# First projection of an MLP in four of six column pairs by seven block products instead of eight

## The chip, the cores and the metric

The kernel runs on one core of a Trainium2 chip. The metric is the device time of one execution in microseconds (us). Five engines work beside each other: TensorE (PE: matmuls; its weight loads are a separate row, PEld), VectorE (DVE), ScalarE (ACT), GpSimd (POOL) and SyncE (SP, which here only issues loads). DMA engines move data and can add into memory while they write ("accumulating" DMA).

## The reference

Three stages, all in float32, for B=2 batches of S=576 tokens (1152 tokens in all) with 8 heads of 64:

```python
# stage 1: linear attention, phi(x) = concat(exp(p), exp(-p)), p = x@w_phi - max|x@w_phi|
kv = einsum('bhsf,bhsd->bhfd', k_p, v);  z = sum(k_p, axis=2)
x = einsum('bhsf,bhfd->bhsd', q_p, kv) / (einsum('bhsf,bhf->bhs', q_p, z)[..., None] + 1e-06)
# stage 2, "first MLP": x [1152, 512], d_ff = 1536
x = (x @ w_a * (x @ w_b)) @ w_out
# stage 3, "second MLP": 4 experts, F = 1024, p = probs normalized over experts
for e in range(4):
    out += p[:, e:e + 1] * (maximum(x @ w1[e], 0) @ w2[e])
```

## The kernel before

**Precision.** A matmul takes its operands in fp32r. Each operand is therefore split into a high part (a copy by ACT that rounds, `high`) and a low part (what is left over, `low`), and a product is three matmuls: high·high, high·low, low·high. The low part is either a subtraction on DVE or POOL, or ("M") a negated copy on ACT followed by an accumulating DMA issued by POOL (L146 and L147).

**Weights.** w_a, w_b and w_out come as 64-bit words that carry float64 values. SP loads them in small pieces (L445); ACT takes magnitude and rest (L467, L468), DVE clamps, shifts and joins them (L475, L478, L481), POOL adds (L484). Then come the high part (L134) and the low part (L135, POOL, or L147). The weights of the second MLP are float32 and need only sums and splits.

**First MLP.** d_ff is cut into six pairs of 256 columns (j = 0 to 5). Pairs 0, 1, 4 and 5 run in halves of 288 tokens: `unit_ab` does w_a (ACT copies the bank to `a`, L755 multiplies by the bank of w_b into `gg`), the product is split into `hhb` (L761 is its low part on DVE), and `o1` (L778 to L780) does the projection back with w_out, which DVE adds to `part` (L672). Pairs 2 and 3 run in blocks of 384 tokens (`block_ab`, L805 to L807, and `block_o`, L834 to L836). Every projection here is plain: all 2×2×2 block products.

**Second MLP.** Also in pairs (j = 0 to 15) and two halves tp of 576 tokens, named unit (j, tp). The first projection goes by seven block products (a Strassen-like scheme): `unit` (L664 to L666) makes products M1 to M7 in banks X, Y, Z from block sums of weights (`wc`) and of x (`xc`, made once by `sums_x`, L383 and L386). ACT copies a bank (L669), DVE adds a bank to the copy (L672), and X is accumulated on in place, so a product into X waits until ACT has copied it. The second projection (L978 to L980) goes by seven too, with sums of h (L918), and DVE accumulates the result times p (L986); pairs in EXCEPT, and only halves named there, are done plainly (L1023 to L1025).

**What sets the order.** TensorE's order is the order of the program's loops: a unit yields after each block product, and `run` puts queued work of the projection back between. The preparation of weights is a list of tasks, of which so many are taken after each product as the tables RATES, TASKS and BEFORE say. In the attention the string SCRIPT orders everything. Each engine runs its own list in order, so an instruction that waits holds back all behind it on that engine.

**Memory at the change of stage.** The order of the last units of the first MLP is (4,0), (5,0), (4,1), then `unit_h(0, 0)` of the second MLP, then (5,1). Only then are the pools of the first MLP released and the second buffer of `wc` and the sums of x for tp = 1 allocated (`l_p`):

```python
        xt_p.release()
        w_p.release()
        ga_p.release()
        l_p = ctx.enter_context(tc.tile_pool(name="l", bufs=1, side="left", reuse_waits="tile"))
        xc[1] = l_p.tile([128, 2, 7, 2, HT], F32R, tag="xc", name="xc")
        wc_t.append(l_p.tile([128, 2, 7, 256], F32R, tag="wc", name="wc"))
```

Of the kernel before, what the change touches and what calls it, by code (L numbers as in the profile page):

```python
# [18 lines left out]
NT = B * S  # L19
# [9 lines left out]
S2 = (0, 1)  # L29
EXCEPT = ((15, 1), (15, 0))  # L30
SUMS_H = "PPDP"
LOW_H = "DDMDDD"
LOW_P = "MDP"
SUMS_1 = "DDDP"
SUMS_2 = "DDPD"
LOW_1 = "PMM"
LOW_2 = "MMMM"
LATE = (4, 6, 9, 9, 11, 12, 12)
SUMS_H1 = "PPDP"
LOW_H1 = "DDPDDD"  # L40
LATE1 = (1, 1, 2, 3, 4, 6, 8)
BEFORE1 = (0, 3, 4, 0, 4, 0, 4, 3, 8, 3, 5, 6, 10, 7, 4, 4)
RATE = 1.8
CAP = 1.6
PLAIN2 = 9
RATE0 = 0.9
RATE9 = 1.4
RATES = (1.3, 1.3, 1.4, 1.8, 2.7)
TASKS0 = (1, 0, 5, 0, 4, 1, 0, 0, 0, 1, 0, 1, 0, 2)
TASKS = (0, 1, 1, 4, 4, 1, 0, 0, 1, 1, 1, 1, 1, 1)  # L50
BEFORE = (0, 2, 4, 3, 4, 3, 2, 3, 8, 5, 5, 7, 10, 0, 1, 4)
PLAIN = (0, 4, 1)
# [26 lines left out]
def tile_linear_attention_then_mlps(ctx, tc, qT, kT, v, w_phi, wab, wout, w12, probs, out):  # L79
# [17 lines left out]
    ab_p = ctx.enter_context(tc.tile_pool(name="ab", bufs=1, side="left"))  # L97
    w_p = tc.alloc_tile_pool(name="w", bufs=1, side="left")
# [7 lines left out]
    ga_p = None  # L106
    l_p = None
# [14 lines left out]
    with tc.manual_schedule():  # L122
# [13 lines left out]

        def engine(by):
            return nc.gpsimd if by == "P" else nc.vector

        def high(hi, src):  # L140
            nc.scalar.activation(out=hi, in_=src, func=AF.Copy)  # L141

        def low(by, lo, src, hi):

            if by == "M":
                nc.scalar.activation(out=lo, in_=src, func=AF.Copy, scale=-1.0)  # L146
                nc.gpsimd.dma_start(out=lo, in_=src, accum_op=ALU.add)  # L147
            else:
                engine(by).tensor_tensor(out=lo, in0=src, in1=hi.bitcast(F32), op=ALU.subtract)  # L149
# [223 lines left out]
        def stage_xparts(b, c, x):  # L373
            xf = x.rearrange("p a b -> p (a b)")
            hi, lo = (t[:, c, S * b:S * b + S] for t in xs)
            nc.scalar.activation(out=hi, in_=xf, func=AF.Copy)
            nc.gpsimd.tensor_tensor(out=lo, in0=xf, in1=hi.bitcast(F32), op=ALU.subtract)

        def sums_x(b, a, second):
# [4 lines left out]

            def high(k, n, src):
                nc.scalar.activation(out=o[:, 0, k:n, a, :], in_=src, func=AF.Copy)  # L386

            def low(k, n, src):
                sub(nc.vector, o[:, 1, k:n, a, :], src, o[:, 0, k:n, a, :].bitcast(F32))

            x, o = part[b][:, a], xc[b]
            end = (b, a) == (B - 1, 1)
            if not second:
                tt[b, a] = m_p.tile([128, 4, HT], F32, tag="g", name="t", bufs=3)
                sub(nc.vector if end else nc.gpsimd, tt[b, a][:, 0], x[:, 0], x[:, 1])
                return
# [25 lines left out]

        raws = {}
        units = []
        for j in range(FP1):
            units += [("ab", 2 * j), ("ab", 2 * j + 1), ("o", j)]
        f64 = [(u, f) for u in units for f in range(2)]
        for j in range(FP2):
            units += [("1", j), ("2", j)]
        f64_next = [0]  # L430

        def load_raw():

            if f64_next[0] >= len(f64):
                return
            u, f = f64[f64_next[0]]
            f64_next[0] += 1
            t = w_p.tile([128, 1024], U32, tag="raw", name="raw", bufs=2)
            src = {"ab": wab, "o": wout}[u[0]][u[1]]
            src = src[:, 512 * f:512 * f + 512].bitcast(U32)  # L440
            if u[0] == "ab":
                for n in range(4):
                    for d in range(2):
                        r = 64 * (n % 2) + 32 * d
                        nc.sync.dma_start(  # L445
                            out=t[32 * n:32 * n + 32].rearrange("p (a d x) -> p a d x", a=2, d=2)[:, :, d],
                            in_=src[r:r + 32].rearrange("p (a e x) -> p a e x", a=2, e=2)[:, :, n // 2],
                        )
            else:
                nc.sync.dma_start(out=t, in_=src)  # L450
            raws[u, f] = t

        w_t = {}
        state = {}


        SPARE = [("ab", FA - 6), ("ab", FA - 5)]

        def begin(k):

            rv = raws[f64[k]].rearrange("p (n t) -> p n t", t=2)
            lo, hi = rv[:, :, 0], rv[:, :, 1]
            m = w_p.tile([128, 512], U32, tag="m", name="m", bufs=2)
            r = w_p.tile([128, 512], U32, tag="rn", name="rn", bufs=2)
            nc.scalar.activation(out=m.bitcast(F32), in_=hi.bitcast(F32), func=AF.Abs)  # L467
            nc.scalar.activation(out=r, in_=lo, func=AF.Copy, scale=2.0 ** -29)  # L468
            state[k] = hi, m, r

        def middle(k):
            hi, m, r = state[k]
            x = w_p.tile([128, 512], U32, tag="wx", name="wx", bufs=2)
            mf = m.bitcast(F32)
            nc.vector.tensor_scalar(  # L475
                out=mf, in0=mf, scalar1=bits(0x38000000), scalar2=bits(0x47EFFFFF), op0=ALU.max, op1=ALU.min
            )
            nc.vector.tensor_scalar(  # L478
                out=m, in0=m, scalar1=3, scalar2=0x3FFFFFFF, op0=ALU.logical_shift_left, op1=ALU.bitwise_and
            )  # L480
            nc.vector.scalar_tensor_tensor(  # L481
                out=x, in0=hi, scalar=0xC0000000, in1=m, op0=ALU.bitwise_and, op1=ALU.bitwise_or
            )
            nc.gpsimd.tensor_tensor(out=x, in0=x, in1=r, op=ALU.add)  # L484
            state[k] = x.bitcast(F32)
            load_raw()

        def parts(k):
            u, f = f64[k]
            if u in SPARE:  # L490
                if u not in w_t:
                    t = m_p.tile([128, 2, 2, 2, 512], F32R, tag="xc", name="w")
                    w_t.update((s, t[:, i]) for i, s in enumerate(SPARE))
            elif f == 0:
                if u[0] == "ab":
                    w_t[u] = ab_p.tile([128, 2, 2, 512], F32R, tag=f"ab{ab_turn[0] % 4}", name="w")
                    ab_turn[0] += 1
                else:
                    w_t[u] = od_p.tile([128, 2, 2, 512], F32R, tag="o", name="w", bufs=2)
            two_parts(w_t[u][:, 0, f], w_t[u][:, 1, f], state.pop(k), nc.gpsimd)  # L500

        stage_t = {}
        ab_turn = [0]

        def load_w(u):


            def go():
                if u == ("1", 0):
                    stage_t[u] = [w_p.tile([128, 4, 256], F32, tag="raw", name="wt", bufs=2) for _ in range(2)]  # L510
                    t = stage_t[u][0]
                elif u[0] == "1":
                    home = 3 if len(S2) == 2 or u[1] % 2 else 1
                    t = ab_p.tile([128, 8, 256], F32, tag=f"ab{home}", name="wt")
                    stage_t[u] = t[:, 0:4], t[:, 4:8]
                else:
                    big = ab_p.tile([128, 8, 256], F32, tag="ab2", name="wx")
                    t = big[:, 0:4].rearrange("p (f h) n -> p f (h n)", f=2)
                    stage_t[u] = t, big
                for f in range(2):  # L520
                    src = w12[2 * u[1] + f]
                    if u[0] == "1":
                        o = t[:, 1:3] if f == 0 else t[:, 0:4:3]
                        for h in range(2):
                            nc.sync.dma_start(
                                out=o[:, h].rearrange("p (a n) -> p a n", a=2),
                                in_=src[:, 0:512].rearrange("p (a h n) -> p h a n", h=2, a=2)[:, h],
                            )
                    else:
                        nc.sync.dma_start(out=t[:, f], in_=src[:, 512:1024])  # L530
            return go

        def sum_w(u, k):
            def go():
                if u[0] == "2":
                    b11, b12, b21, b22, t0, t1, t2, t3 = (stage_t[u][1][:, n] for n in range(8))
# [704 lines left out]
```

## Time and profile before

| | |
|---|---|
| median of three runs | 689.53 us (689.14 to 691.02) |
| profiled execution | 691.6 us, its span 689.7 us |
| instructions | 15326 |
| PE busy | 679.0 us, 98% of the span |
| DVE / ACT / POOL busy | 542.8 (79%) / 427.6 (62%) / 334.9 (49%) us |

The span is the time between the first and last instruction on the core; what lies around it is 1.9 us here. Matmuls overlap each other in the records: one of 288 columns is shown as 0.29 us long, while the next starts 0.13 us later. So the cost of a matmul is read from start to start, not from its length. The attention takes about the first 90 us, the first MLP the time to about 335, the second MLP the rest.

### The profile page before, as it was taken

The numbers are of one execution on the slowest core, as the hardware profiler recorded it, in microseconds if no ns is written. First come the engines' busy times: TensorE is split into PE (matmuls) and PEld (weight loads), VectorE is DVE, ScalarE is ACT, GpSimd is POOL, SyncE is SP. The second block draws the span as 40 slices with busy tenths as digits, with TensorE's granted clock in tenths as the row PEclk, the third lists the DMA queues.
The fourth block names the chain that finished last, engine by engine and source line by source line (L and its number), as shares of the span: only waits on it lengthen the run. The fifth ranks groups of instructions, "written<-read, shape, count | busy, mean of one in ns | idle before, by whom it ended". The sixth has DMA issues, their size and how long they took to land.

```text
span 689.7 us, 15326 instructions
## 1 busy us (share of the span) xinstructions
PE 679.0 (98%) x5706; PEld 653.9 (95%) x5706; DVE 542.8 (79%) x1175; ACT 427.6 (62%) x907; POOL 334.9 (49%) x354
## 2 busy tenths in 40 slices
PE   9998999999999999999899999999999999999998
PEld 8995679999999999999799999999999999999996
DVE  6889964547565567564649999999999999999985
ACT  5767855454444353433597777777686868777761
POOL 1211664334443344511256756665665667565730
PEclk9999999999999999999999999999999999999999
DMA  6742232223322232211257656665656666665654
GB/s 196 211 130 69 59 98 62 68 86 82 105 73 80 92 93 62 62 31 32 40 122 139 132 112 127 128 129 114 129 122 120 129 133 119 125 126 115 124 85 153
DMA packets 63499, 72.63 MB, mean 105 GB/s; under 512 B 7296, under 2 KB 43456, under 8 KB 63424
## 3 DMA queue, kind: packets, MB, share of 16 engines
q0 software_dynamic: 15552, 26.48, 22.9%
q1 hardware_dynamic: 47648, 45.00, 21.9%
q8 instruction: 45, 0.74, 0.5%
q14 instruction: 30, 0.25, 0.1%
q10 hardware_dynamic: 224, 0.16, 0.1%
HBM read 42.78 MB, written 2.36 MB: 65 GB/s over the span
## 4 chain that ended last, share of the span: by engine, by line
PE 93%; DVE 4%; ACT 1%; issue 1%; DMA 1%; SPq 0%; DVEq 0%
PE kv L276 5%; PE ab L748 5%; PE X L665 5%; PE X L666 5%; PE ab L750 5%; PE ab L749 5%; PE X L664 5%; PE X L980 4%; PE X L978 4%; PE X L979 4%; PE num L343 3%; PE acc L779 3%; PE acc L780 2%; PE acc L778 2%; PE Z L666 2%; PE Z L664 2%
## 5 line engine op out<-in xcount | busy, mean ns | idle before, releaser
L986 DVE SCALAR_TENSOR_TENSOR oacc<-X,pr,oacc 128x256 f32<-128x256 f32 x224 | 97.1, 474 | 5.4 <-PE X L980 5.2
L484 POOL TENSOR_TENSOR wx<-wx,rn 128x512 uint32<-128x512 uint32 x36 | 46.5, 1291 | 92.1 <-DVE wx L481 92.1
L918 POOL TENSOR_TENSOR h<-h 128x256 f32<-128x256 f32 x56 | 44.5, 794 | 82.3 <-DVE h L918 49.6
L135 POOL TENSOR_TENSOR w<-wx,w 128x512 fp32r<-128x512 f32 x36 | 47.9, 1332 | 70.5 <-ACT w L134 70.5
L665 PE MATMUL X<-xc,wc 128*128 128x288 f32 x256 | 75.7, 296 | 0.0
L748 PE MATMUL ab<-xh,w 128*128 128x288 f32 x256 | 75.7, 296 | 0.0
L666 PE MATMUL X<-xc,wc 128*128 128x288 f32 x256 | 75.5, 295 | 0.0
L750 PE MATMUL ab<-xh,w 128*128 128x288 f32 x256 | 75.4, 295 | 0.0
L749 PE MATMUL ab<-xl,w 128*128 128x288 f32 x256 | 75.4, 294 | 0.0
L664 PE MATMUL X<-xc,wc 128*128 128x288 f32 x256 | 75.3, 294 | 0.0
L669 ACT ACTIVATE h<-X 128x288 f32<-128x288 f32 x64 | 26.3, 410 | 69.7 <-PE X L666 69.7
L141 ACT ACTIVATE hhs<-h 128x256 fp32r<-128x256 f32 (+2 forms) x146 | 65.1, 475 | 0.3 <-DVE h L918 0.2
L147 POOL DMA_DIRECT2D w<-wx x60 | 51.9, 877 | 26.1 <-ACT w L146 16.2
L980 PE MATMUL X<-w,hhs 128*128 128x256 f32 x224 | 63.2, 282 | 0.2 <-DVE hhs L149 0.2
L978 PE MATMUL X<-w,hhs 128*128 128x256 f32 x224 | 62.8, 280 | 0.2 <-DVE oacc L986 0.2
L979 PE MATMUL X<-w,hhs 128*128 128x256 f32 x224 | 62.9, 281 | 0.0
L149 DVE TENSOR_TENSOR hhs<-h,hhs 128x512 fp32r<-128x512 f32 x114 | 60.4, 529 | 0.8 <-ACT hhs L141 0.8
L672 DVE TENSOR_TENSOR part<-acc,part 128x288 f32<-128x288 f32 (+2 forms) x80 | 34.7, 452 | 31.6 <-PE acc L836 18.6
L986 DVE SCALAR_TENSOR_TENSOR oacc<-Z,pr,oacc 128x256 f32<-128x256 f32 x112 | 48.8, 476 | 8.1 <-PE Z L980 7.1
L664 PEld LDWEIGHTS X<-xc,wc 128*128 128x128 f32 x256 | 48.3, 189 | 0.3
L665 PEld LDWEIGHTS X<-xc,wc 128*128 128x128 f32 x256 | 48.2, 188 | 0.4
L748 PEld LDWEIGHTS ab<-xh,w 128*128 128x128 f32 x256 | 48.0, 188 | 0.5 <-issue 0.5
(153 smaller groups left out, 2386.5 us busy)
## 6 DMA issues: line engine op xcount, KB each, us to landing
w<-wx POOLq DMA_DIRECT2D x60, 256.0 KB, 4.3
raw<-in_wab SPq DMA_DIRECT2D x192, 64.0 KB, 2.1
wt<-in_w SPq DMA_DIRECT2D x64, 128.0 KB, 2.6
wc<-wt POOLq DMA_DIRECT2D x32, 256.0 KB, 3.3
wx<-in_w SPq DMA_DIRECT2D x32, 256.0 KB, 3.1
raw<-in_wout SPq DMA_DIRECT2D x12, 512.0 KB, 3.7
xraw<-in_qT SPq DMA_DIRECT2D x6, 384.0 KB, 4.0
v<-in_v SPq DMA_DIRECT2D x8, 256.0 KB, 5.2
```

The costliest lines, as they stand in the source:

```text
L141: nc.scalar.activation(out=hi, in_=src, func=AF.Copy)
L149: engine(by).tensor_tensor(out=lo, in0=src, in1=hi.bitcast(F32), op=ALU.subtract)
L664: nc.tensor.matmul(out=ps, lhsT=whi, rhs=xhi, start=first and a == 0, stop=False, skip_group_check=True)
L665: nc.tensor.matmul(out=ps, lhsT=whi, rhs=xlo, start=False, stop=False, skip_group_check=True)
L666: nc.tensor.matmul(out=ps, lhsT=wlo, rhs=xhi, start=False, stop=a == 1, skip_group_check=True)
L748: nc.tensor.matmul(out=t, lhsT=whi, rhs=hi, start=(c == 0), stop=False)
L749: nc.tensor.matmul(out=t, lhsT=whi, rhs=lo, start=False, stop=False)
L750: nc.tensor.matmul(out=t, lhsT=wlo, rhs=hi, start=False, stop=(c == KD - 1))
L978: nc.tensor.matmul(out=t[:, p], lhsT=hi, rhs=whi, start=st, stop=False, skip_group_check=True)
L979: nc.tensor.matmul(out=t[:, p], lhsT=hi, rhs=wlo, start=False, stop=False, skip_group_check=True)
L980: nc.tensor.matmul(out=t[:, p], lhsT=lo, rhs=whi, start=False, stop=True, skip_group_check=True)
L986: nc.vector.scalar_tensor_tensor(out=o, in0=t[:, p], scalar=pr[:, i, e:e + 1], in1=o, op0=ALU.mult, op1=ALU.add)
```

## The change

Four of the six pairs of the first MLP (2 to 5) make x @ w_a by seven block products with `unit`, the code of the second MLP. For that the attention stage is followed by block sums of x (`sums_t`: four differences per 288-token plane, split in high and low), and each of these pairs' w_a gets four block sums (`split`). w_b stays plain, pairs 0 and 1 stay plain. The 384-token blocks are gone: all units are halves of 576 tokens in two 288-token parts. In a pair the order is a of half 0, a of half 1, b of half 0, b of half 1; in the last pair a, b of half 0 and then a, b of half 1. `unit_h(0, 0)` comes after both.

Memory is laid out anew: two staging buffers (`st_p`), three buffers wA, wB and wC for loads and conversion, one home `wc_t[0]` for w_a and one `wc_t[1]` for w_b, which become the two `wc` buffers of the second MLP. Low parts of converted weights are now nearly all made with the accumulating DMA (LOWS). Preparation is a list per engine (tables PLAIN, POPS, ENG, H00). In the second MLP fewer low parts of h are made on DVE and more by accumulating DMA (LOW_H, LOW_H1), and unit (1, 0) joins EXCEPT: its second projection is plain. SCRIPT orders the attention stage otherwise, with eight instead of nine conversions before the last piece of x.

```diff
-EXCEPT = ((15, 1), (15, 0))
+SEVEN = {1: "", 2: "a", 3: "a", 4: "a", 5: "a"}
+SUMS = {"a": "DDDD", "b": "PPDP", "1": "DDPP", "2": "DDDP"}
+LOWS = {"a": "MMD", "b": "MMD", "1": "DMM", "o": "MM", "2": "PMMM"}
...
+EXCEPT = ((15, 1), (15, 0), (1, 0))
...
+        def minus(o, i, e):
+
+            if e == "M":
+                nc.scalar.activation(out=o, in_=i, func=AF.Copy, scale=-1.0)
+
+        def rest_of(o, i, hi, e):
+            if e == "M":
+                nc.gpsimd.dma_start(out=o, in_=i, accum_op=ALU.add)
+            else:
+                by[e].tensor_tensor(out=o, in0=i, in1=hi.bitcast(F32), op=ALU.subtract)
...
+            raws = [wide["wA"][:, 0:1024], wide["wA"][:, 1024:2048], wide["wB"][:, 0:1024]]
+            ms = [wide["wB"][:, 1024 + 512 * n:1536 + 512 * n] for n in range(2)]
+            ms += [wide["wC"][:, 512 * n:512 * n + 512] for n in range(2)]
+            return raws[k % 3], ms[k % 4]
...
+            if m in "ab":
+                gate = (m, j - 1) if j > 1 else "m" if m == "b" else None
+            s = []
+            for k in range(4):
...
+                h = op("A", u, high(lo, hi, LOWS[m][n]), *after, gate=gate)
...
+                q = late_op(LOWS[m][n], u, low(lo, hi, LOWS[m][n]), h)
+                last = [q] if n == 0 else last + [q]
...
+                tt["x", b, a] = x, t
+                xh, xl = planes()[:2]
+                nc.vector.tensor_tensor(out=x, in0=xh.bitcast(F32), in1=xl.bitcast(F32), op=ALU.add)
+
+            def diff(k):
+                def go():
+                    x, t = tt["x", b, a]
+                    i, j = ((x[:, 0], x[:, 1]), (x[:, 2], x[:, 0]), (x[:, 2], t[:, 0]), (x[:, 3], t[:, 2]))[k]
+                    by[DIFFS[k]].tensor_tensor(out=t[:, k], in0=i, in1=j, op=ALU.subtract)
+                return go
+
...
-            w, x = w_t[u], xc[tp]
+            w, x = w_t[u], (xq[tp], xt[tp], u[0] != "1")
...
+        def unit_a(j, tp):
+            if "a" not in SEVEN[j]:
+                return unit_pa(j, tp)
+            need(("t", tp))
+            c = ca[tp] = new_c("a")
+            return unit(("a", j), tp, c, nothing, nothing, lambda X: copy(c[:, 1, HT:], X))
...
-        order = [(0, 0), (1, 0), (0, 1), (1, 1)] + [(j, n) for j in BLOCKS for n in range(NTB)]
-        order += [(FP1 - 2, 0), (FP1 - 1, 0), (FP1 - 2, 1), None, (FP1 - 1, 1)]
-        for jt in order:
-            if jt is None:
-                run(unit_h(0, 0), 1.2, RATES[4])
-                continue
-            j, tp = jt
-            if j in BLOCKS:
...
-        l_p = ctx.enter_context(tc.tile_pool(name="l", bufs=1, side="left", reuse_waits="tile"))
-        xc[1] = l_p.tile([128, 2, 7, 2, HT], F32R, tag="xc", name="xc")
-        wc_t.append(l_p.tile([128, 2, 7, 256], F32R, tag="wc", name="wc"))
-        w2_t.extend(l_p.tile([128, 8, 256], F32R, tag=f"w2{k}", name="w") for k in range(2))
...
+        run(unit_plain(1), 1.0, PLAIN)
+        for j in range(1, FP1):
+            for m, tp in (("a", 0), ("a", 1), ("b", 0), ("b", 1)) if j < FP1 - 1 else (("a", 0), ("b", 0), ("a", 1), ("b", 1)):
+                k = m if m in SEVEN[j] else m.upper()
+                run((unit_a if m == "a" else unit_b)(j, tp), R5 if (j, tp) == (FP1 - 1, 1) else POPS[k], ENG[k])
+                if j == FP1 - 1 and m == "b":
+                    fresh(tp, True)
+        assert not any(t == 0 for q in queue for t, l, h in q[1])
```

GpSimd at the passage from the first to the second MLP, before: `wt_3873` are the staged weights of pair 1 of the second MLP, `wc_4146` their split home, `t_4182` sums of x for tp = 1.

```order
L543 TENSOR_TENSOR wt_3873<-wt_3873 128x256
L383 TENSOR_TENSOR t_4182<-part_2183 128x288
L383 TENSOR_TENSOR t_4182<-part_2183,t_4182 128x288 x2
L149 TENSOR_TENSOR wc_4146<-wt_3873,wc_4146 128x768
L147 DMA wc_4146<-wt_3873 128x512 x2
L543 TENSOR_TENSOR wx_4070<-wx_4070 128x256
L147 DMA w_4148<-wx_4070 128x512 x4
```

The same place now; `wt_4118` and `wc_1616` are the staged and split weights of that pair, and `t_4186` are the last sums of x.

```order
L375 TENSOR_TENSOR t_3964<-part_1619,t_3964 128x288 x2
L375 TENSOR_TENSOR t_4019<-part_1619 128x288
L375 TENSOR_TENSOR t_4019<-part_1619,t_4019 128x288 x2
L447 DMA wc_105<-wt_3399 128x512 x2
L666 TENSOR_TENSOR wt_4118<-wt_4118 128x256 x2
L375 TENSOR_TENSOR t_4186<-part_1959 128x288
L375 TENSOR_TENSOR t_4186<-part_1959,t_4186 128x288 x2
L447 DMA wc_1616<-wt_4118 128x512 x2
L776 TENSOR_TENSOR wt_4123<-wt_4123 128x256
```

The two DMAs into the home of pair 1 now stand behind the sums of x for tp = 1 and two weight sums, with no subtraction of 768 columns before them.

ScalarE at that place before; `h_4266` is the copy of unit (0, 0), `h_4335` of unit (0, 1).

```order
L669 ACTIVATE h_4266<-X_4267 128x288
L141 ACTIVATE wc_4146<-wt_3873 128x768
L669 ACTIVATE h_4266<-Z_4269 128x288
L872 ACTIVATE hhb_1578<-h_4266 128x288
L141 ACTIVATE wc_4146<-wt_3873 128x512
L146 ACTIVATE wc_4146<-wt_3873 128x512
L872 ACTIVATE hhb_1578<-h_4266 128x576
L872 ACTIVATE hhb_1578<-X_4267 128x288
L141 ACTIVATE wc_4146<-wt_3873 128x512
L146 ACTIVATE wc_4146<-wt_3873 128x512
L669 ACTIVATE h_4335<-X_4336 128x288
```

And now; `h_4106` is unit (0, 0), `oacc_4258` belongs to the second projection of unit (0, 0), and `h_4301` is unit (0, 1).

```order
L883 ACTIVATE h_4106<-X_4107 128x288
L883 ACTIVATE h_4106<-Z_4109 128x288
L677 ACTIVATE wc_1616<-wt_4118 128x768
L1136 ACTIVATE hhb_1530<-h_4106 128x288
L1136 ACTIVATE hhb_1530<-h_4106 128x576
L381 ACTIVATE xq_4104<-part_1959 128x3x288
L677 ACTIVATE wc_1616<-wt_4118 128x512
L443 ACTIVATE wc_1616<-wt_4118 128x512
L1136 ACTIVATE hhb_1530<-X_4107 128x288
L381 ACTIVATE xt_4105<-t_4186 128x4x288
L677 ACTIVATE wc_1616<-wt_4118 128x512
L443 ACTIVATE wc_1616<-wt_4118 128x512
```

The last split of the weights of pair 1 (L146 before, L443 now) stood directly ahead of the first copy of unit (0, 1). Now two splits of x and two rows of `oacc` follow it, and only then the first copy of unit (0, 1), `h_4301`.

VectorE in pair 2, before: `gg` and `hhb` of one block, `part` of the projection back.

```order
L672 TENSOR_TENSOR part<-acc,part 128x384
L475 TENSOR_SCALAR m<-m 128x512
L478 TENSOR_SCALAR m<-m 128x512
L481 SCALAR_TENSOR_TENSOR wx<-raw,m 128x512
L812 TENSOR_TENSOR gg<-ab,a 128x384
L817 TENSOR_TENSOR hhb<-gg,hhb 128x384
L672 TENSOR_TENSOR part<-acc,part 128x384 x2
```

And now in pair 3, with names as before; `c<-Y`, `c<-X`, `c<-Z` are additions of the seven-product unit.

```order
L886 TENSOR_TENSOR part<-acc,part 128x288 x3
L582 SCALAR_TENSOR_TENSOR wB<-wA,wB 128x512
L886 TENSOR_TENSOR part<-acc,part 128x288 x2
L563 TENSOR_SCALAR wB<-wB 128x512
L569 TENSOR_SCALAR wB<-wB 128x512
L886 TENSOR_TENSOR c<-Y,c 128x288
L449 TENSOR_TENSOR hhb<-c,hhb 128x576
L886 TENSOR_TENSOR part<-acc,part 128x288
L582 SCALAR_TENSOR_TENSOR wB<-wB 128x512
L886 TENSOR_TENSOR part<-acc,part 128x288
L886 TENSOR_TENSOR c<-X,c 128x288
L886 TENSOR_TENSOR c<-Z,c 128x288
```

Between two conversions (three instructions each) there now stand additions of the unit and of the projection back mixed.

## Rows read from the trace of the kernel before

**Rows 1.** Busy time (count) by engine in stretches, granted clock, DMA share, GB/s.
```profile
50.00:64.00 14.00, 11.55 (x208) 8.55 (x204) 13.12 (x24) 11.47 (x28) 2.57 (x2) 1.00 0.30 95
...
160.00:170.00 10.00, 9.55 (x59) 9.10 (x58) 6.01 (x8) 4.64 (x9) 4.69 (x4) 1.00 0.35 93
170.00:290.00 120.00, 120.00 (x782) 120.00 (x782) 74.78 (x150) 52.89 (x96) 53.01 (x43) 1.00 0.30 84
...
330.00:341.00 11.00, 8.93 (x62) 8.29 (x62) 8.86 (x17) 8.08 (x16) 4.19 (x4) 1.00 0.14 25
341.00:345.00 4.00, 4.00 (x16) 3.41 (x16) 0.76 (x2) 0.41 (x1) 0.13 (x1) 0.58 0.53 113
...
368.00:686.00 318.00, 318.00 (x2429) 312.49 (x2428) 299.15 (x726) 228.81 (x520) 193.06 (x231) 1.00 0.60 124
```

**Rows 2.** Groups by line and shape: TensorE; busy us, mean ns, idle before.
```profile
L748 PE MATMUL ab<-xh,w 128*128 128x288 f32 x256 | 75.7, 296 | 0.0
...
L778 PE MATMUL acc<-hhb,w 128*128 128x288 f32 x128 | 37.9, 296 | 0.1
...
L805 PE MATMUL ab<-xh,w 128*128 128x384 f32 x96 | 32.2, 336 | 0.0
...
L834 PE MATMUL acc<-hhb,w 128*128 128x384 f32 x48 | 16.0, 334 | 0.0
```

**Rows 3.** Timeline of TensorE: start, duration, line, operation.
```profile
299.80 0.29 PE L664 MATMUL Z<-xc,wc 128*128 128x288 f32 x1
...
302.98 0.29 PE L664 MATMUL Z<-xc,wc 128*128 128x288 f32 x1
...
230.34 0.34 PE L805 MATMUL ab<-xh,w 128*128 128x384 f32 x1
...
233.49 0.34 PE L805 MATMUL ab<-xh,w 128*128 128x384 f32 x1
...
341.65 0.63 PE L1023 MATMUL acc<-w,hhb 128*128 128x512 f32 x1
...
344.21 0.38 PE L664 MATMUL X<-xc,wc 128*128 128x288 f32 x1
...
677.92 0.39 PE L1023 MATMUL acc<-w,hhs 128*128 128x512 f32 x1
...
684.72 0.28 PE L1023 MATMUL acc<-w,hhs 128*128 128x256 f32 x1
...
686.03 0.28 PE L1025 MATMUL acc<-w,hhs 128*128 128x256 f32 x1
```

**Rows 4.** Chain that ended last, 334 to 347 us: start, us, what.
```profile
336.55 0.53 ACT wc L146
...
337.36 3.32 DMA wc<-wt
...
340.72 0.41 PE Z L666
```

**Rows 5.** Groups by line and shape: GpSimd and ScalarE.
```profile
L147 POOL DMA_DIRECT2D w<-wx x60 | 51.9, 877 | 26.1 <-ACT w L146 16.2 <-PE Z L980 3.2 <-issue 3.1
...
L669 ACT ACTIVATE h<-X 128x288 f32<-128x288 f32 x64 | 26.3, 410 | 69.7 <-PE X L666 69.7
...
L543 POOL TENSOR_TENSOR wt<-wt 128x256 f32<-128x256 f32 x16 | 14.4, 902 | 2.6 <-DVE wt L543 2.6
```

**Rows 6.** Timeline of VectorE, then of GpSimd, from 155.7 us.
```profile
155.71 0.42 DVE L475 TENSOR_SCALAR m<-m 128x512 f32<-128x512 f32 x1
...
157.66 1.36 DVE L475 TENSOR_SCALAR m<-m 128x512 f32<-128x512 f32 x1
...
157.45 1.27 POOL L484 TENSOR_TENSOR wx<-wx,rn 128x512 uint32<-128x512 uint32 x1 [5.62 <-DVE wx L481]
```

**Rows 7.** DMA issues: tile, engine, count, KB each, median us to landing.
```profile
w<-wx POOLq DMA_DIRECT2D x60, 256.0 KB, 4.3
...
wc<-wt POOLq DMA_DIRECT2D x32, 256.0 KB, 3.3
```

More of the change, by code (lines that the diff above doesn't have):

```diff
@@ L421, in tile_linear_attention_then_mlps @@
         kept_low = []
+        ticks = [0]
         raws = {}
[L424 to L451, printed above, removed]
@@ L453, in tile_linear_attention_then_mlps @@
+        f64 = [((m, j), f) for j in range(FP1) for m in "abo" for f in range(2)]
+        f64.sort(key=lambda uf: (uf[0][1], "abo".index(uf[0][0]), uf[1]))
+        late = [(m, j) for j in range(FP2) for m in "12"]
         w_t = {}
         state = {}
[L457 to L469, printed above, removed]
@@ new lines, in tile_linear_attention_then_mlps, with place, freed, op @@
+        uses = {}
+        recent = {"st": [], "raw": []}
+        bufs = {"st": 2, "m": 4, "raw": 3}
+        made = {}
+        m_rel = {}
+        def place(tag, k):
+            made[tag] = k
+            return k
+        def freed(tag):
+            return recent[tag][-bufs[tag]] if len(recent[tag]) >= bufs[tag] else None
+        def op(e, u, fn, *after, gate=None):
+            ops.append((u, fn, [a for a in after if a is not None], gate, e))
+            line[e].append(len(ops) - 1)
+            return len(ops) - 1
@@ new lines, in ready, with emit, prep @@
+        def ready(k, steps):
+            u, fn, after, gate, e = ops[k]
+            free = gate is None or (m_p is not None if gate == "m" else uses[gate] == 0)
+            return free and all(a in at and (at[a] + steps * (2 if ops[a][4] == "S" or a in slow else 1) <= ticks[0] or ops[a][4] == e) for a in after)
+        def emit(k):
+            ops[k][1]()
+            at[k] = ticks[0]
+        def prep(engines):
+            for e in engines + "XXSS":
+                k = next((k for k in line[e] if ready(k, 1)), None)
+                if k is not None:
+                    line[e].remove(k)
+                    emit(k)
@@ L505, in load_w @@
         def load_w(u):
             def go():
[L509 to L519, printed above, removed]
+                t = st_p.tile([128, 8, 256], F32, tag="st", name="wt", bufs=2)
@@ L599, in tile_linear_attention_then_mlps @@
-        t_next = [0]
-        before = {}
-        for kinds, n in (("ab",), 4), (("o", "2"), 2):
-            same = [u for u in units if u[0] in kinds and u not in SPARE]
-            before.update({u: same[i - n] for i, u in enumerate(same) if i >= n})
-        before["load", "2", 0] = ("ab", FA - 4)
-        before["load", "1", 1] = ("ab", FA - 3)
-        before["load", "2", 1] = ("ab", FA - 2)
-        before["load", "1", 2] = ("ab", FA - 1)
-        for j in range(2, FP2):
-            before["1", j] = ("1", j - 2)
@@ L611, in tile_linear_attention_then_mlps @@
[L611 to L628 removed]
+                second(u, l, gate)
@@ L827, in block_o @@
[L827 to L842 removed]
+        left = {}
```

768 lines of the change are left out of this document (481 added, 287 removed).

## The prediction

> **What bounds the kernel now.** I read the stretches of the span first, because a change in the first MLP has its price there and not in the mean over the span. TensorE is busy for all of the 120 us from 170 to 290 and for all of the 318 us from 368 to 686 [rows 1]. In these stretches only fewer or shorter matmuls can save time. The reader should look for the stretches in which it is not full: 50 to 64 us, where VectorE is busy 13.12 of 14 us and TensorE 11.55; 160 to 170 (0.45 us idle); and 330 to 341 (2.07 us idle), behind which lie 4 us at a granted clock of 0.58 [rows 1]. Then I read the groups by shape for the number of matmuls [rows 2], the timeline for what each costs from start to start [rows 3], and the chain for what the idle 2 us wait for [rows 4].
>
> The costs by [rows 3]: 24 steps of 288 columns lie between 299.80 and 302.98, 0.1325 us each; 18 of 384 columns between 230.34 and 233.49, 0.175 us; 30 of 512 between 677.92 and 684.72, 0.2267 us; 11 of 256 between 684.72 and 686.03, 0.119 us.
>
> **Term 1, the matmuls: -5.2 us.** One pair's x @ w_a by halves is 4 token parts × 2 column blocks × 4 row blocks × 3 = 96 matmuls of 288 columns. By seven products it is 84. Four pairs save 48, and 48 × 0.1325 = 6.4 us. The 384-column work is 3 × 96 + 3 × 48 = 432 matmuls [rows 2], 75.6 us at 0.175; the same columns as 576 matmuls of 288 cost 76.3, so +0.7. Unit (1, 0) of the second MLP loses 42 matmuls of 256 columns (5.0 us) and gets 24 of 512 (5.4), so +0.4. All this lies on an engine that was full, so it counts in full: -6.4 + 0.7 + 0.4 = -5.3, or -5.2 without rounding in between. If TensorE stays full, this term can't come out otherwise.
>
> **Term 2, the passage to the second MLP: -3.8 us.** In the chain ScalarE ends the last split of pair 1's weights at 337.08, GpSimd issues the accumulating DMA, that takes 3.32 us, and TensorE's product Z starts at 340.72 [rows 4]. The wait is the 2.07 us of the stretch. After it the clock is at the lower level for part of 341 to 345: mean 0.58 of full, that is 4 × 0.42 = 1.7 us lost, and six matmuls of 512 columns take 2.56 us from 341.65 to 344.21, 0.43 each in place of 0.227 [rows 1, 3]. Fully granted it is 2.4 GHz; 0.43 is what the level of 1.2 GHz gives. Both together are 3.8 us. The weights came late because their home was free only when the first MLP's buffers were released. Now the home of w_b becomes that buffer, and is free after the last w_b unit. The split is written inside unit (0, 0), and in ScalarE's and GpSimd's lists the DMA stands well ahead of unit (0, 1): by the matmuls in between (some 40 of 288 columns and 24 of 512 of the plain part: 5.3 + 5.4 = 10.7 us), some 10 us for a DMA that lands in 3.3 us [rows 7]. Bounds: 0 (another wait takes its place, with the same dip of the clock) to -3.8. I take -3.8, since both the wait and the work ahead of it are in rows.
>
> **Term 3, the attention: -0.4 us.** From 50 to 64 us VectorE is the bound [rows 1]. The new order has one conversion fewer there on VectorE and one clamp on GpSimd; the clamp alone is 0.42 us [rows 6]. What else the conversions saved there is done later beside matmuls. At most the 2.45 us idle in that stretch can go; at worst GpSimd's clamp, with no row of its own, takes as long as its other operations on 512 columns, 1.27 us [rows 6], and is waited for, +1.3. I take the clamp.
>
> **Term 4, new waits in the first MLP: +0.6 us.** VectorE gets more work: its instructions of the first MLP go from 219 to 304. It was busy 74.8 of 120 us with 150 instructions, 0.50 us each [rows 1]; 85 more are 42 us over the some 235 us of that stage, so its share goes from 62% to about 80%. ScalarE was at 44% and gains the block sums' splits and the negated copies; I put these at a third of its work, which makes some 60%. Neither is full, but a seven-product unit has a shorter rope than a plain one: product M6 or M7 goes into the bank that ScalarE must have copied, with one product Y (6 × 0.1325 = 0.8 us) and at times a projection back (another 0.8) in between, and the copy takes 0.41 [rows 5]. A ScalarE instruction that waits for a raw load and stands ahead of the copy holds it back; behind the copy wait VectorE's additions and then TensorE. The eight units of pairs 2 to 5 are bounded by nothing at all below and by a wait like that of the passage, 2.07 us each, above: 0 to 16.6 us. The nearest row for a wait in the middle of this stage is 160 to 170, 0.45 us for one [rows 1], with VectorE's stretched conversion in front of it. I take one matmul, 0.13 us, per unit, 1.0 in all, less the 0.45 of that place whose order is gone: +0.6.
>
> **Term 5, the second MLP: 0.** TensorE is full there; GpSimd was busy 193 of 318 us [rows 1]. It now issues 146 accumulating DMAs rather than 106, 40 × 0.877 = 35 us more, and makes 45 weight sums rather than 29, 16 × 0.90 = 14 us more [rows 5]; what else moves about cancels. That makes 242 of some 318 us, 76%. VectorE falls from 299 us by about as much as it makes fewer low parts, so its 94% goes down. The cover is TensorE's own work: a pair of units is some 21 us long (318 us for 15 pairs), while GpSimd has some 16 us to do in it. Bounds: 0 to +15 (second rival).
>
> **Sum.** -5.2 - 3.8 - 0.4 + 0.6 = -8.8. Of the profiled execution's 691.6 us (span 689.7) that leaves 682.8 (span 680.9). That execution lies 2.1 us above the median of the runs, 689.53, so for the median I expect 680.7, and say 681.
>
> Where VectorE and GpSimd meet, the trace speaks against the change: a clamp of 0.42 us took 1.36 us when it started at 157.66, inside a GpSimd operation that ran from 157.45 to 158.72 [rows 6]; it ended 0.30 us after that one. The Trainium skill, "SBUF — State Buffer", section "SBUF: two separate sides", says that the two engines take a shared pair of ports as an exclusive lock for a whole instruction, and warns that a DMA issued by GpSimd waits for its descriptors while VectorE holds it. The row agrees with the first half; no run here shows the second. By this rule the 40 added DMA issues of the second MLP would be slowed too, and the time would come out as in the second rival.
>
> **Rivals.**
> (a) The passage's wait only moves. Unit (0, 1) then waits for sums of x or for other weights, and the clock dips again. For it: the last sums of x for half 1, partly on GpSimd, can begin only after the last projection back, and VectorE was busy 8.86 of 11 us there [rows 1]. Against it: all other weights are issued early. Time: 689.5 - 5.2 - 0.4 + 0.6 = 684.5; with half of it back, 682.6.
> (b) Slower: low parts that come late in the second MLP. Place: the second projection of each unit, whose low parts of h now come in more cases by a DMA that GpSimd issues behind sums and other DMAs. A DMA lands 3.3 to 4.3 us after its issue [rows 7], where VectorE passes over 512 columns in 0.42 us (its clamp) [rows 6]. If GpSimd falls behind by the stretching seen in [rows 6], the price is about half a microsecond in each of some 29 units, +14.5, and the time 695.2. It decides from 8.8 / 29 = 0.3 us per unit. Against it: GpSimd has a quarter of its time free, and the projection is not asked for until some products later.
> (c) Waits eat the gain of the first MLP. At a microsecond in each of eight units in place of 0.13, term 4 is 7.6, and the time 687.7; with two, it is about 695, slower as well. For it: VectorE at 80% with conversions that hold up additions; against it: four banks, and TensorE full through 120 us with VectorE at 62% [rows 1].
>
> **How the numbers follow.** Forecast (677.5 to 683.5): 0.55. Rival (a) (683.5 to 686.5): 0.20. Rival (c): 0.13, of which 0.07 within 0.3% of 689.53 (2.07 us, about what can be told from no change), 0.03 on either side. Rival (b): 0.12, of which 0.11 slower and 0.01 the same. So faster is 0.55 + 0.20 + 0.03 = 0.78, the same 0.08, slower 0.14. The range is 677 to 689: its low end has the attention's whole 2.45 us and no new waits (689.5 - 5.2 - 3.8 - 2.5 = 678) and another microsecond for stretches that I count full; its upper end takes in (a) and the first half of (c).
>
> **What would show it.** Right: 336 seven-product matmuls in the first MLP at 0.13 us each; no wait of TensorE for `wc` near the passage, and a clock of 1.0 there; TensorE full from the start of the second MLP on, GpSimd at about three quarters. Term 4 shows as idle time of TensorE before products into X and Z with ScalarE or VectorE as the one that ended it. The prediction is wrong if TensorE's idle time within the second MLP is above 2 us, or if the clock is lowered anywhere else, since a dip costs as much again as the wait ahead of it.

## The result and the profile after

The changed kernel took 683.38 us (median of 4 runs, 682.83 to 684.04), the kernel before 689.5 us in the runs beside it. The ratio is 0.9907, 95% interval 0.9889 to 0.9926, a gain of 6.1 us. It is faster, inside the stated range, and 2.4 us above the 681 us forecast. In the two profiled executions the span fell from 689.7 to 681.1 us, by 8.6 us, close to the 8.8 us of the sum. So the question is not where a large gain went, but why the traces show 8.6 us and the medians some 6, and whether the terms are right one by one.

The head of the page of the changed kernel: busy time, share of the span, instructions.

```profile
span 681.1 us, 15846 instructions
## 1 busy us (share of the span) xinstructions
PE 671.9 (99%) x5784; PEld 646.5 (95%) x5784; DVE 574.2 (84%) x1159; ACT 458.4 (67%) x990; POOL 389.3 (57%) x425
```

The same kernel by stretches, with columns as in [rows 1] (PE, PEld, DVE, ACT, POOL, granted clock, DMA share, GB/s). The second MLP ends some 9 us earlier than before (its last matmul starts at 677.33 instead of 686.03), so 330 to 366 holds the passage, and 370 to 677 answers to 368 to 686.

```profile
50.00:64.00 14.00, 12.18 (x212) 8.54 (x212) 12.70 (x22) 11.57 (x28) 0.00 (x0) 1.00 0.23 65
160.00:170.00 10.00, 10.00 (x77) 10.00 (x76) 5.99 (x14) 4.91 (x10) 3.44 (x4) 1.00 0.71 152
170.00:290.00 120.00, 120.00 (x906) 120.00 (x905) 91.29 (x182) 59.32 (x110) 43.24 (x38) 1.00 0.52 120
330.00:366.00 36.00, 36.00 (x230) 33.24 (x229) 21.27 (x40) 28.43 (x64) 23.85 (x28) 1.00 0.52 99
366.00:370.00 4.00, 2.89 (x24) 2.69 (x23) 3.90 (x8) 2.83 (x7) 4.00 (x6) 1.00 0.99 192
370.00:677.00 307.00, 307.00 (x2337) 301.15 (x2337) 285.61 (x635) 226.22 (x531) 240.62 (x283) 1.00 0.67 125
```

TensorE is full through the first MLP and through the passage, at full clock: the 2.07 us wait and the dip of [rows 1, 4] are gone. VectorE rose from 62% to 76% in 170 to 290, GpSimd from 61% to 78% in the second MLP. But a new hole of 1.11 us stands at 366 to 370. The chain of waits in that place (start, us, what) shows what it is:

```profile
363.29 0.37 POOL xq L447
363.66 0.16 issue
363.82 5.40 DMA hhs<-h
369.21 0.04 issue
369.26 0.39 PE Z L1243
```

The low part of a block of h, made by an accumulating DMA, lands 5.40 us after its issue, and the third matmul of product Z waits for it. When it is issued, two others of the same queue are still under way: one with weights (w, 256 KB), which lands 0.08 us later, and one for other blocks of h (xq, 128 KB). And 0.34 us behind it SyncE issues two loads of the next weights (256 KB each); from 366 to 370 us the DMA engines are 99% busy (the share 0.99 above). That is the place of rival (b), in one unit of some 29.

```profile
364.16 1.06 SPq L762 DMA_DIRECT2D wt<-in_w  x2
```

### The profile page after: what moved, and what is told of

The parts are those of the page before. It is cut to its first block, busy times and chain, and to the rows that moved or that the text cites. A ratio compares the mean times of both kernels' runs of the same rounds, so it can differ in the third digit from the quotient of the medians.

```text
span 681.1 us, 15846 instructions
## 1 busy us (share of the span) xinstructions
PE 671.9 (99%) x5784; PEld 646.5 (95%) x5784; DVE 574.2 (84%) x1159; ACT 458.4 (67%) x990; POOL 389.3 (57%) x425
## 4 chain that ended last, share of the span: by engine, by line
PE 89%; DMA 3%; POOL 2%; SPq 2%; DVE 2%; ACT 1%; issue 1%; POOLq 0%; ACTq 0%; DVEq 0%
PE X L879 6%; PE X L880 6%; PE X L878 6%; PE ab L1029 4%; PE acc L1089 4%; PE ab L1031 4%; PE acc L1088 4%; PE ab L1030 4%; PE acc L1087 4%; PE X L1242 4%; PE X L1241 4%; PE X L1243 4%; PE Z L878 3%; PE Z L879 3%; PE Z L880 3%; PE num L336 2%
## 5 line engine op out<-in xcount | busy, mean ns | idle before, releaser
L878 PE MATMUL X<-xt,wc 128*128 128x288 f32 x240 | 71.0, 296 | 0.0
L879 PE MATMUL X<-xt,wc 128*128 128x288 f32 x240 | 70.8, 295 | 0.0
L880 PE MATMUL X<-xt,wc 128*128 128x288 f32 x240 | 70.8, 295 | 0.0
L447 POOL DMA_DIRECT2D hhs<-h x41 | 57.3, 1398 | 12.6 <-ACT hhs L443 10.4
L447 POOL DMA_DIRECT2D wc<-wt x40 | 35.5, 889 | 45.4 <-ACT wc L443 25.7
L1029 PE MATMUL ab<-xq,wc 128*128 128x288 f32 x192 | 56.8, 296 | 0.0
L1089 PE MATMUL acc<-hhb,w 128*128 128x288 f32 x192 | 56.8, 296 | 0.0
L1030 PE MATMUL ab<-xq,wc 128*128 128x288 f32 x192 | 56.7, 295 | 0.0
L1088 PE MATMUL acc<-hhb,w 128*128 128x288 f32 x192 | 56.7, 295 | 0.0
L1031 PE MATMUL ab<-xq,wc 128*128 128x288 f32 x192 | 56.5, 294 | 0.0
L1087 PE MATMUL acc<-hhb,w 128*128 128x288 f32 x192 | 56.5, 294 | 0.0
L886 DVE TENSOR_TENSOR part<-acc,part 128x288 f32<-128x288 f32 x80 | 35.2, 453 | 19.7 <-PE acc L1089 19.3
L447 POOL DMA_DIRECT2D w<-wt x46 | 46.8, 1314 | 1.0 <-issue 1.0
L878 PEld LDWEIGHTS X<-xt,wc 128*128 128x128 f32 x240 | 45.2, 188 | 0.4
L879 PEld LDWEIGHTS X<-xt,wc 128*128 128x128 f32 x240 | 45.1, 188 | 0.2
L880 PEld LDWEIGHTS X<-xt,wc 128*128 128x128 f32 x240 | 45.1, 188 | 0.0
L883 ACT ACTIVATE hhs<-h 128x256 fp32r<-128x256 f32 (+2 forms) x100 | 41.8, 442 | 1.3 <-DVE h L1181 0.9
L677 ACT ACTIVATE wc<-wt 128x512 fp32r<-128x512 f32 (+1 forms) x60 | 41.6, 693 | 0.0
```

What stands on the lines that cost most here:

```text
L447: nc.gpsimd.dma_start(out=o, in_=i, accum_op=ALU.add)
L878: nc.tensor.matmul(out=ps, lhsT=whi, rhs=xhi, start=first and a == 0, stop=False, skip_group_check=True)
L879: nc.tensor.matmul(out=ps, lhsT=whi, rhs=xlo, start=False, stop=False, skip_group_check=True)
L880: nc.tensor.matmul(out=ps, lhsT=wlo, rhs=xhi, start=False, stop=a == 1, skip_group_check=True)
L883: nc.scalar.activation(out=o, in_=i, func=AF.Copy)
L1029: nc.tensor.matmul(out=t, lhsT=whi, rhs=hi, start=(c == 0), stop=False)
```

## The experiments

Each was timed against the kernel before, on the same chip and in turns, in three groups: the changed kernel again, before again, two_seven and ab25; low6d, a1, lowm and ab3; low6p, tailp, early_v and three.

**The changed kernel again**

> The changed kernel once more, against the kernel before on the same chip. Theory A (the profiled execution of before, 691.6 us, was a long one; its passage wait and clock dip of 3.8 us are not in every execution): the median gain stays near 6 us, ratio about 0.991. Theory B (the gain is the 8.6 us by which the two traces' spans differ, and the medians of few runs hid it): ratio about 0.9875, 680.9 us.

684.16 us (5 runs) against 690.96 (19 runs): ratio 0.9915, interval 0.9901 to 0.9928. The interval lies clear of the 0.9875 of theory B. Its trace has a span of 682.4 us and two waits of the new kind instead of one:

```profile
PE Z L1243 <- DMA hhs<-h: 2.4, 2, 1.3
...
PE kv L270 <- DMA v<-in_v: 0.7, 1, 0.7
```

(columns: engine, line, what it waited for, us in total, times, the longest.) The second stands at 482 us, a hole that was 0.2 us long in the first trace.

**The kernel before again**

> The kernel before once more, for its trace. Theory A: its span comes out 1 to 3 us shorter than 689.7 us, and the trace has a smaller wait for the weights wc at 337 to 341 us, or no granted clock below 1.0 behind it. Theory B: the same wait of 2.07 us and the same dip as in the first trace, span 689.5 to 690.

690.9 us, ratio 1.0003 (0.9992 to 1.0013). Its trace has a span of 689.1 us. By stretches, and then the chain:

```profile
330.00:341.00 11.00, 9.54 (x64) 8.77 (x62) 8.85 (x20) 8.92 (x16) 3.30 (x4) 1.00 0.13 23
341.00:345.00 4.00, 3.40 (x19) 3.06 (x20) 1.66 (x2) 0.79 (x3) 1.03 (x2) 1.00 0.40 68
```

```profile
338.26 3.30 DMA wc<-wt
341.56 0.04 issue
341.60 0.40 PE Z L666
...
342.00 0.14 PE Z L664
```

The wait is there again: 1.46 us idle before 341 and 0.60 behind it, 2.06 in all, for the same DMA. The clock is not lowered: the next matmul of 288 columns starts 0.14 us after the one before, where the first trace had 0.24. So the wait is in both executions and the dip in one of two. The 1.7 us of the dip are not to be counted on. Theory A holds in this point, though not in the span, which is 0.6 us shorter and not 1 to 3.

How often the dip comes can be read from the mean granted clock that is on record for each run. The 19 runs of before in this group fall into nine at 689.3 to 690.0 us and ten at 691.0 to 691.4. All nine have a clock of 0.999 or 1.0, and all ten have 0.997 or 0.998, as the first trace with its dip has (0.997). The runs of before in the other two groups divide in the same way: 24 of all 47 have the lower value, and each of these is slower than each of the rest. So about half of the executions have the dip, and it accounts for the step of some 1.5 us between their times; that it stands at the passage in the untraced runs too is taken from the one trace that has it. The trace without the dip is of a run of 690.87, which is long for another reason: 0.8 us more idle time in the attention than the first (TensorE busy 19.12 instead of 19.95 of the 20 us from 10 to 30).

**Seven products in two pairs only**

```diff
-SEVEN = {1: "", 2: "a", 3: "a", 4: "a", 5: "a"}
+SEVEN = {1: "", 2: "", 3: "", 4: "a", 5: "a"}
```

> Only pairs 4 and 5 make x @ w_a by seven products; 2 and 3 plain: 24 matmuls of 288 columns more, with less work on VectorE. Theory full (TensorE is full, so a matmul saved counts whole): 24 x 0.1325 = 3.2 us slower than the changed kernel. Theory eaten (seven-product units bring waits that take part of the gain, a microsecond a unit): under 1 us slower or even faster.

686.74 us, ratio 0.9955 (0.994 to 0.997): 2.6 us slower than the changed kernel in the same group, span 685.0 against 682.4. It has 24 more plain matmuls. Full predicted 3.2, eaten under 1. Theory full holds; the 0.6 us that are missing are within the spread of both.

**w_b by seven in pairs 2 to 5, in pair 3, and w_a of pair 1**

```diff
-SEVEN = {1: "", 2: "a", 3: "a", 4: "a", 5: "a"}
+SEVEN = {1: "", 2: "ab", 3: "ab", 4: "ab", 5: "ab"}   # ab25
+SEVEN = {1: "", 2: "a", 3: "ab", 4: "a", 5: "a"}      # ab3
+SEVEN = {1: "a", 2: "a", 3: "a", 4: "a", 5: "a"}      # a1
```

> Pairs 2 to 5 make x @ w_b by seven products too: 48 matmuls fewer than the changed kernel, four more sets of weight sums and eight more units with additions on VectorE and ScalarE, by the changed kernel's own tables. Theory full: 6.4 us faster, about 677 us, if VectorE (81% busy in this stage by the changed kernel's trace, some 92% then) still keeps up. Theory eaten: VectorE, ScalarE or the splits of w_b come late, waits of over 0.8 us in each of the eight units, no gain or slower, with idle TensorE ahead of products into X and Z.

> Only pair 3 makes x @ w_b by seven products beside the four w_a: 12 matmuls fewer than the changed kernel, and the second MLP's lists stay as they are. Theory full: 1.6 us faster. Theory eaten (as the kernel with all four w_b showed, each such unit waits about a microsecond for the copy on ScalarE): two units x 1.0 us, so 0 to 2 us slower.

> Pair 1 makes x @ w_a by seven products too: 12 matmuls of 288 columns fewer than the changed kernel; the second MLP stays as it is. Theory full: 12 x 0.1325 = 1.6 us faster. Theory eaten: pair 1 comes while VectorE is busiest (55.2 of 66 us from 94 to 160), and has to wait for the block sums of x: waits of over a microsecond, no gain.

ab25: 726.33 us, ratio 1.053 (1.0511 to 1.0549). ab3: 685.13, 0.9921 (0.9903 to 0.9939). a1: 710.63, 1.0279 (1.0254 to 1.0305). The waits of TensorE in ab25, then in a1:

```profile
PE Z L1243 <- DMA hhs<-h: 14.8, 12, 1.8
PE X L878 <- ACT c L883: 8.0, 8, 2.7
PE X L880 <- DMA wc<-wt: 3.6, 1, 3.6
```

```profile
PE X L880 <- DMA wc<-wt: 10.1, 3, 8.7
PE X L878 <- ACT wc L677: 5.8, 1, 5.8
PE X L878 <- ACT c L883: 3.3, 3, 1.8
```

In ab25 there are eight waits for the copy of X, one microsecond each on the mean, which is the price of rival (c). The 14.8 us for hhs belong to the second MLP, where the tables put GpSimd's DMAs in another order than in the changed kernel. So this run mixes two things, with three stretches of lowered clock besides, and only ab3, which leaves the second MLP's lists as they are, prices the units themselves. Here the two units lose 1.24 and 1.21 us (time beyond the pace of their matmuls), and save 0.8 each. The median is 1.0 us above that of the changed kernel, as this would make it, but the intervals overlap. Its timeline of TensorE, then of ScalarE, in the first of them:

```profile
215.65 0.29 PE L880 MATMUL Y<-xq,wc 128*128 128x288 f32 x1
216.61 0.40 PE L878 MATMUL X<-xt,wc 128*128 128x288 f32 x1 [0.67 <-ACT c L883]
```

```profile
214.69 0.84 ACT L677 ACTIVATE wc<-wt 128x768 fp32r<-128x768 f32 x1
215.42 0.83 ACT L443 ACTIVATE wc<-wt 128x768 fp32r<-128x768 f32 x1
216.16 0.40 ACT L883 ACTIVATE c<-X 128x288 f32<-128x288 f32 x1
```

The copy of X stands behind two splits of the next weights, 1.5 us of ScalarE, where product Y covers only 0.8. So a seven-product unit gains here only where no such split stands ahead of its first copy. In the changed kernel's w_a units the lists keep this clear; that their tables do so, not that w_a differs from w_b, is argued and not shown. In a1 the weights of pair 1 are simply not there yet: TensorE waits 5.8 us for their split and right after it 8.7 us for their accumulating DMA. No wait for the block sums of x shows, the other half of that expectation.

**Where the low parts of h are made**

```diff
-LOW_H = "DMPDDM"
-LOW_H1 = "DPMDMM"
+LOW_H = "MMMMMM"; LOW_H1 = "MMMMMM"    # lowm
+LOW_H1 = "DPMDDM"                      # low6d: block 6 on VectorE
+LOW_H1 = "DPMDPM"                      # low6p: block 6 on GpSimd
+LOW_H = "DMPDDP"; LOW_H1 = "DPMDMP"    # tailp: the tails on GpSimd
```

> Changed kernel with every low part of h in the seven-product units of the second MLP by accumulating DMA (LOW_H and LOW_H1 all M). It takes some 6 subtractions a pair off VectorE and GpSimd and puts as many DMAs on GpSimd's queue. Theory queue (low parts that come late through one queue set the time, the slower rival of the prediction): waits of a microsecond or more in most of 29 units, 15 to 40 us slower than the changed kernel. Theory slack (the queue has room, TensorE asks for low parts late enough): within 2 us of it.

893.61 us, ratio 1.2933 (1.2908 to 1.2957), 209 us slower than the changed kernel was in the first group. Theory queue holds in kind and is far too small in size:

```profile
PE X L1243 <- DMA hhr<-h: 61.3, 14, 5.4
PE Z L1243 <- DMA hhs<-h: 47.4, 13, 4.4
PE X L1241 <- DVE oacc L1249: 22.6, 13, 2.5
```

A wait for a DMA here is 3.6 to 4.4 us on the mean, and TensorE's granted clock over the span is 0.903. That is at most 0.097 × 893.9 = 87 us; as the three waits shown take 131 of the 209 us, the clock's part is below 80, the rest of the lowered stretches being waits anyway.

> Changed kernel, but the low part of block 6 of h (tokens of half 1, table LOW_H1, fifth letter M to D) is a subtraction on VectorE instead of an accumulating DMA, in 14 units. Theory queue (the waits of 1.1 to 1.3 us for hhs at 367 us and, in the second trace, at 481 us come because this DMA is queued behind the weights' DMAs): both waits go, 1.2 to 2.5 us faster than the changed kernel, about 682 us beside 684.2. Rival DVE (VectorE is 93% busy there, and 14 x 0.45 = 6.3 us more make it late elsewhere): no gain, with TensorE waiting for oacc or h.

691.03 us, ratio 1.0011 (1.0 to 1.0021), 7 us slower than the changed kernel, against the gain that theory queue forecast. The waits for hhs are gone, but TensorE is late by small amounts at the same two places of nearly every pair of units, 0.45 and 0.15 us beyond its pace. Of these the profile shows the first as idle time:

```profile
PE X L1241 <- DVE oacc L1249: 3.4, 12, 0.3
```

```profile
370.00:684.00 314.00, 310.48 (x2317) 299.08 (x2316) 295.62 (x644) 220.84 (x517) 228.32 (x268) 1.00 0.61 117
```

The 14 subtractions add about 6.3 us (14 × 0.45) to VectorE, and the time grows by about as much. It is the rival DVE, and stronger than it was put: VectorE, at 93% in the changed kernel, had no room for them. Whether it is its share that counts or the place of this subtraction in its list, ahead of the reads of the banks (oacc), no run separates.

> Changed kernel, but the low part of block 6 of h (half 1, LOW_H1 fifth letter M to P) is a subtraction on GpSimd instead of an accumulating DMA. GpSimd's own time stays (0.94 us for such a subtraction, 0.9 to 1.2 for the issue of the DMA), VectorE gets nothing. Theory queue (the two waits of 1.1 to 1.3 us are the DMA's place in its queue): both go, no new ones, 1.2 to 2.5 us faster than the changed kernel (684.2). Rival load (GpSimd as such is late): the same waits stay, now with POOL as the one that ended them.

681.2 us, ratio 0.9866 (0.985 to 0.9881), below the interval of the changed kernel (0.9901 to 0.9928). The same edit on the engine that has room removes the waits for hhs and adds next to none; all that TensorE waits for behind the attention is

```profile
PE X L1243 <- DVE hhr L449: 0.2, 1, 0.2
```

```profile
370.00:677.00 307.00, 305.93 (x2327) 299.84 (x2325) 285.00 (x635) 221.64 (x518) 237.00 (x282) 1.00 0.63 121
```

(of the 1.07 us that are not busy, 0.2 are this wait; the rest is the end, as the last matmul now ends ahead of 677). So it is this one DMA that costs TensorE the 1.1 to 2.4 us of the two traces, and GpSimd's load as such nothing that shows. This run takes the DMA away altogether, so it does not show why it was late, and its place in the queue, the reason of theory queue, does not explain it alone. In the first trace of the changed kernel the same DMA of the unit at 478 us has the same two under way ahead of it, and the one with the weights lands later than at 364 us, 0.91 us behind its issue in place of 0.08. Yet it lands after 3.57 us, and the profile shows no idle time before product Z:

```profile
478.33 1.15 POOL L447 DMA_DIRECT2D hhs<-h  x1
...
479.45 0.82 SPq L762 DMA_DIRECT2D wt<-in_w  x2
```

What differs is how soon SyncE's two loads follow: 1.12 us behind it here, 0.34 us at 363.82. In the second trace, where TensorE waits in this unit too, they come 0.79 us behind it and it takes 4.74 us. The seven traces that make this low part by DMA in the changed kernel's order (all such but ab25) have 98 of these transfers. The 16 with the loads up to 0.6 us behind took 5.04 us at the median, the 41 with 0.95 to 1.15 us 4.18, the 16 with 1.35 us or more 3.24. So the loads that run beside it are the likelier reason. No run moved them, so this is read from traces and not tested. Nor is the queue's order free: in ab25 another transfer of weights (wc) stands directly ahead, and most of these DMAs take 4.2 to 5.5 us.

> Changed kernel, but the low parts of the tail of h (both halves, sixth letter M to P) are subtractions on GpSimd, 0.6 to 0.76 us, instead of DMAs of 256 pieces of 256 bytes, whose issue holds GpSimd 1.2 to 2.6 us. Theory queue: block 6 is issued before the tail, so its wait at 367 us stays, at most the one at 481 us goes: 0 to 1.3 us faster. Rival load: GpSimd gains some 20 us in all, and both waits go, up to 2.5 us faster.

684.19 us, ratio 0.9915 (0.9893 to 0.9937), no change. One wait for hhs of 0.9 us is left, that of block 6 at 368 us. So the DMAs of the tail, which are issued behind it, are not what it waits for; the loads of SyncE come 0.25 us behind it here, and it takes 5.15 us.

**The load of v earlier, and all three edits**

```diff
-SCRIPT = "VPtt1Pt1x2Re3xexkxe3tktPe2kkPxt3e2x32x3v2ek..."
+SCRIPT = "VPtt1vPt1x2Re3xexkxe3tktPe2kkPxt3e2x32x32ek..."
```

> Changed kernel, but the first load of v of batch 1 is issued ahead of eight weight loads on SyncE's queue, by some 4 us. In the traces TensorE waits 0.7 to 2.1 us for it at 29 us in some executions and not in others. Theory v (this wait is most of the spread between executions): it goes, and the median is 0.7 to 1 us lower than that of the changed kernel. Rival: the load of k behind it comes as much later and TensorE waits for that: no change.

683.4 us, ratio 0.9901 (0.9886 to 0.9917). The wait for v is gone from the trace; two waits for hhs (1.9 us) are there. 0.8 us lower than the changed kernel of the first group, as theory v says, but the intervals overlap, so it is not shown.

> All three edits together. If each wait is gone and nothing takes its place: 2 to 3.5 us faster than the changed kernel, 680.5 to 682, a ratio of 0.986 to 0.988 to the kernel before. If the waits only move: within 1 us of the changed kernel, 0.991.

681.9 us, ratio 0.9883 (0.9867 to 0.99). It is faster than the changed kernel, and not faster than the edit of block 6 alone; the intervals of the two overlap. The lowest median of the study is that of low6p: one letter.

## Why the prediction was right, and where a term was not

**Term 1 (-5.2) was right.** TensorE's instructions went from 5706 to 5784, as the counts of the term make it; the count by pace is 5.2 us less, and the run with two pairs shows that the matmuls count nearly whole.

**Term 2 (-3.8) was right in its mechanism and too large by up to 1.7.** The wait went and none came in its place, against rival (a). But half of the term was the dip of the clock, read from one execution. The kernel before has the same wait without a dip in another. So the term is -2.1 in such executions and -3.8 in the others, about half and half. To subtract the sum from one profiled execution's 691.6 us and then carry the difference over to the median was the step that failed here: the execution was one with the dip. The forecast took the dip off twice, once in the term and once in the 2.1 us by which that execution lay above the median. From a median without the dip the same sum gives 689.5 - 5.2 - 2.1 - 0.4 + 0.6 = 682.4, where 683.4 was measured.

**Term 3 (-0.4) had the right sign and is smaller than the spread.** From 50 to 64 us TensorE's idle time fell from 2.45 to 1.82 us, but the second trace of before has 1.87 there as well. The change brought a wait for v of 0.7 to 1.0 us in its two traces, which I had not looked for. The whole start up to 150 us, before, before again and after:

```profile
0.00:150.00 150.00, 145.63 (x1856) 130.47 (x1857) 110.97 (x190) 93.24 (x191) 55.71 (x47) 1.00 0.38 112
0.00:150.00 150.00, 144.37 (x1849) 129.12 (x1850) 110.89 (x190) 92.38 (x189) 55.76 (x47) 1.00 0.39 109
0.00:150.00 150.00, 145.42 (x1861) 130.08 (x1862) 126.62 (x208) 107.05 (x220) 55.46 (x50) 1.00 0.56 138
```

Both traces of the changed kernel have 1861 matmuls by then, wait for v included. That is 5 and 12 more than before, all of 288 columns at that place, or 0.7 and 1.6 us.

**Term 4 (+0.6) was of the wrong sign.** From 90 to 330 us TensorE was idle 0.47 us before and 0.07 us after. VectorE did rise to about the share I forecast (186.1 of these 240 us, 78%), and ScalarE to 57%, but no unit waited. With a split in front of the copy (ab3) it is 1.2 us a unit, inside the bound of 2.07; single waits of up to 2.7 us in ab25 are beyond it.

**Term 5 (0) was the term that missed.** I took TensorE's own work as the cover of all low parts, by GpSimd's share of time. That share came out as forecast (78% for 76%). What counts is not the share but when one DMA lands: it took 5.40 us where I had 3.3 to 4.3, with the same DMAs ahead of it as in units where it took 3.6, and with two loads of SyncE close behind it. One or two units wait 1.1 to 1.3 us, so the term is +1.1 to +2.4, and the second trace, with 2.4 us, is beyond the 2 us of idle time that I had given as a sign of being wrong. I also said that VectorE's share of 94% would go down; it went to 93%, and low6d found no room there.

So the terms as measured, for the first pair of traces: -5.2 - 3.8 - 0.7 - 0.4 + 1.1 = -9.0, where the spans differ by 8.6; for the second pair: -5.2 - 2.1 - 1.6 - 0.4 + 2.4 = -6.9, where they differ by 6.7. The medians show -6.1 and -6.8. That the first spans came so near to the 8.8 us of the sum is in part luck: term 4 was 1.0 us too high and term 5 1.1 us too low. Rival (b) had the right place and happened in one or two of 29 units. Its price of half a microsecond was too small where it happens, and with every low part on the queue it is 3.6 to 4.4 us a wait and the clock besides.

## What to carry to other kernels

Take from the full engine what you can count, and count it whole; but read a wait and a lowered clock in more than one execution before you put them into a sum for the median. Where a change moves work to DMAs, look at which other transfers, of other engines' queues too, are under way beside the one that is needed first, not at the mean load of the issuing engine. Before you move work to an engine that is as busy as VectorE was here (93%), count it in full: six microseconds of work cost seven, and the same low parts on an engine at 78% gained three.

## What the runs showed of the hardware

An idle stretch of TensorE of the same length (2.06 and 2.07 us) in the same place was followed by the lower clock (1.2 GHz) in one execution and not in the other, and the runs' clocks put it at 24 of 47. The 1.1 to 1.3 us waits of the changed kernel were followed by full clock in both traces. In ab25 waits of 2.7, 3.6 and 1.8 us were followed by the lower clock and one of 2.4 us was not: the length of a wait alone does not tell.

The issue of an accumulating DMA holds GpSimd for 0.877 us on the mean in [rows 5]. After the change the recorded mean is longer:

```profile
L447 POOL DMA_DIRECT2D hhs<-h x41 | 57.3, 1398 | 12.6 <-ACT hhs L443 10.4 <-ACT w L799 2.1
...
L447 POOL DMA_DIRECT2D w<-wt x46 | 46.8, 1314 | 1.0 <-issue 1.0
```

(busy us, mean ns, idle before.) The first row mixes two shapes: 27 of its 41 issues are those of the tail, with 256 pieces in place of 128, and with nothing of the queue under way an issue of 256 pieces takes 1.22 us (median of 17) and one of 128 pieces 0.87 (median of 26). Records of neighbours on GpSimd overlap as well, so part of it may be how they are recorded; the lengths alone cost no time that these runs show.

The Trainium skill, "SBUF — State Buffer", section "SBUF: two separate sides", warns that GpSimd cannot write the descriptors of such a DMA while VectorE runs an instruction in a mode that takes the ports that the two share. A long record does not need that here. In the run with every low part by DMA (lowm) an issue of the tail takes 1.90 us and the next one 1.20, and VectorE is idle beside the long one: it waits from 403.76 to 409.67 us for TensorE. Whether VectorE lengthens other issues no run tells.

```profile
404.74 1.90 POOL L447 DMA_DIRECT2D hhs<-h  x1
412.33 1.20 POOL L447 DMA_DIRECT2D hhs<-h  x1 [5.70 <-ACT hhs L883]
...
409.67 0.88 DVE L1249 SCALAR_TENSOR_TENSOR oacc<-X,pr,oacc 128x256 f32<-128x256 f32 x2 [5.91 <-PE X L1243]
```
